# The late stages of a fused attention and gated-MLP training step rebuilt around crossbar loads and tile-wise buffer reuse

## The chip, the cores and the metric

The kernel runs on one core of one Trainium2 chip; the rounds ran on several chips, so ratios are always to the kernel before in the same rounds. The metric is device time in microseconds (us), median of several executions.

## The reference, cut to what matters

Sequence S = 2048, model width D = 576, H = 32 heads of 128, MLP width F = 4608, all bf16. The kernel computes the output of this step and its eight gradients in one launch.

```python
xn  = layernorm(x)
s   = attention(xn @ wq, k_cache, v_cache) @ wo          # O is (S, H*128)
g   = silu((sigmoid(xn @ w_gate) * (xn @ w_up)) @ w_down)
out = x + s * g
# then the vjp of out with grad_out, for x, k_cache, v_cache, wq, wo, w_gate, w_up, w_down
```

## The kernel before: the parts that matter

The program runs in stages, one after another, each with TensorE (PE) as the main engine:

1. gate/up: `xn @ w_gate`, `xn @ w_up`, with `a = sigmoid(g)` and `h = u*a` stored to HBM,
2. down projection,
3. attention forward and backward, head by head,
4. output projection O wo, then `ds`-related elementwise work that makes `doB`, the gradient at the MLP output,
5. MLP gradients, in 18 blocks of 256 columns of F: `dh`, then `du`, `dg`, and the products for dW_down, dW_up, dW_gate,
6. dWo and dWq, in 8 groups of four heads,
7. dx, in 8 blocks of 256 rows, from `du`, `dg` and `dq`.

Gate/up makes `1 - a` by a second sigmoid and stores the product `b = h*(1-a)`, which stage 5 reads back:

```python
nc.scalar.activation(a_row[:, cs], g_ps[:], AF.Sigmoid)
oma = tmpp.tile([P, FCH], bf, name="oma")
nc.scalar.activation(oma[:], g_ps[:], AF.Sigmoid, scale=-1.0)
...                                                      # cut
nc.vector.tensor_tensor(b_row[:, cs], h_row[:, cs], oma[:], op=ALU.mult)
```

The output projection loads `wo` only after attention, turns O on TensorE, and turns the last 64 columns of `B_w_down` on TensorE too (`ldT_tmp`):

```python
nc.sync.dma_start(t_[:], on2_d[st_ * P:(st_ + 1) * P, :])                 # onr
...                                                                      # cut
for j in range(n):
    nc.tensor.transpose(pt[:, j, :], onr[:, (g + j) * P:(g + j + 1) * P], ident[:])
alt.copy(oT[:, g:g + n, :], pt[:, :n, :])
...                                                                      # cut
nc.tensor.matmul(accs[j][:, :nn], lhsT=oT[:, h, :], rhs=wo_sb[:, h, n0:n0 + nn], ...)
```

The MLP gradients form dW_up and dW_gate in the orientation of the output, with 256 moving columns; dWq does the same with 512 columns, per group of four heads:

```python
for i, (d0, kd) in enumerate(dts):                       # five row tiles of D
    for st in range(NT):                                 # 16 tiles of S
        nc.tensor.matmul(acc[:kd, :], lhsT=xn_all[:, st, d0:d0 + kd], rhs=blk_[:, st, :], ...)
...                                                      # cut: stage 6
nc.sync.dma_start(onb[:], on2_d[:, cols]...)             # 2 MB per group, rows of 1 KB
nc.sync.dma_start(dqb[:], dq2_d[:, cols]...)
if hg == min(2, H // HG - 1): load_T_rows(nc, wuT_sb, B_w_up, D)      # crossbar, 5.3 MB
if hg == min(4, H // HG - 1): load_T_rows(nc, wgT_sb, B_w_gate, D)
```

## Time and profile before

The median was 5324.54 us when the prediction was made (3 executions) and 5319.72 us with the profiled one (4 executions, 5310.42 to 5330.38). These are the page's first lines: busy time of TensorE, its share of the span and its instructions.

```profile
span 5319.7 us, 130025 instructions
...
PE 5076.7 (95%) x54342; PEld 3664.5 (69%) x55220; DVE 2681.6 (50%) x6832; ACT 2629.3 (49%) x4678; POOL 920.6 (17%) x1458
```

TensorE is the bound, so a gain must come from fewer or cheaper matmuls or from the 5% in which it waits. The windows view of the kernel before gives the late stages: output projection, MLP gradients, the wait after them, dWo/dWq, dx. Its columns are the stretch, its length, busy time of each engine with instructions in brackets, then the granted TensorE clock, the share of time that the DMA engines were busy, and GB/s.

```profile
core 0: us, PE busy (x) PEld busy (x) DVE busy (x) ACT busy (x) POOL busy (x), PEclk, DMA share, GB/s
3706.00:3951.00 245.00, 185.81 (x1619) 113.47 (x1648) 76.01 (x124) 43.71 (x67) 35.77 (x44) 0.87 0.51 163
3951.00:4600.00 649.00, 637.42 (x5423) 496.10 (x5477) 251.86 (x708) 146.34 (x415) 180.90 (x270) 0.99 0.53 177
4600.00:4617.00 17.00, 0.64 (x3) 0.34 (x4) 0.00 (x0) 0.36 (x1) 0.54 (x1) 0.58 1.14 312
4617.00:4890.00 273.00, 264.10 (x1632) 128.09 (x1662) 28.44 (x52) 24.43 (x52) 39.12 (x72) 0.99 0.58 179
4890.00:5320.00 430.00, 407.04 (x3261) 210.91 (x3326) 45.93 (x128) 13.39 (x64) 8.63 (x16) 0.98 0.71 147
```

The output projection is the weak one: TensorE is busy for 186 of 245 us there. The waits view tells what TensorE waited for (us in total, times, longest), first in gate/up, then from the end of attention on.

```profile
PE g_ps L393 <- ACT oma L399: 21.7, 20, 2.3
```

```profile
PE pt L86 <- DMA ldT_tmp<-in_B_w_down_dram: 23.9, 1, 23.9
PE acc L902 <- DMA onb<-on_d: 16.5, 2, 16.4
PE pt L805 <- ACT oT L40: 15.0, 13, 1.2
...
PE pt L805 <- DVE oT L42: 7.4, 14, 0.6
...
PE accd L860 <- DMA h_blk<-h_d: 5.1, 1, 5.1
```

Four costs stand here that the change means to remove: the second sigmoid (21.7 us), the load of `ldT_tmp` after attention (23.9), the copies of the turned O (15.0 and 7.4), and the wait for `onb` (16.5). Where the last one comes from is seen in the DMA queue of SyncE in the kernel before, around the end of the MLP gradients at 4599.8 us. The columns are the start, how long the entries took in the queue, and what they moved:

```profile
4582.85 0.36 SPq L886 DMA_DIRECT2D ds_all<-ds_d  x1
4583.26 24.68 SPq L92 DMA_TRANSPOSE wuT_sb<-in_B_w_up_dram  x3
4608.25 0.36 SPq L891 DMA_DIRECT2D onb<-on_d  x1
```

The source asks for these weights with the third head group. The scheduler (see below) had put three of the loads ahead of `onb` already here, and one of them waited 13.6 us for the last copy of the stage before. So `onb` was issued 8.5 us after the last matmul of that stage.

### The profile page before, as it was taken

What the parts mean: (1) busy time and instruction counts of PE and PEld (TensorE: products, weight loads), DVE (VectorE), ACT (ScalarE), POOL (GpSimd) and SP (SyncE); (2) the same over time, 40 slices, a digit from 0 to 9 for tenths busy, and PEclk for the clock granted to TensorE, in tenths of its full rate; (3) what the DMA queues carried; (4) which work ended last, traced back from release to release, by engine and by line L of the source; (5) the groups of instructions that cost most, each with busy time, mean ns of one, the idle gap of its engine ahead of it and who ended that gap; (6) DMA issues with size and microseconds to landing.
All of it is one profiled execution on the core that took longest, in us unless ns stands there. A gap on an engine that the chain in (4) does not pass through costs nothing.

```text
span 5319.7 us, 130025 instructions
## 1 busy us (share of the span) xinstructions
PE 5076.7 (95%) x54342; PEld 3664.5 (69%) x55220; DVE 2681.6 (50%) x6832; ACT 2629.3 (49%) x4678; POOL 920.6 (17%) x1458
## 2 busy tenths in 40 slices
PE   8899999999999999999999999998889999899999
PEld 3345777777877877777777777777557777544454
DVE  5744666666665665665665665665334334210011
ACT  7641766766766666666666666665112222100000
POOL 2222111111111111111111111111112232111000
PEclk9999999999999999999999999999899999999999
DMA  7867999999999999999999999999644555765775
GB/s 297 287 208 171 210 203 210 209 210 204 212 213 201 210 207 191 209 211 203 210 200 197 210 213 206 200 201 217 188 153 166 176 185 174 214 197 132 164 149 109
DMA packets 2724762, 1053.95 MB, mean 198 GB/s; under 512 B 2524913, under 2 KB 2645362, under 8 KB 2722114
## 3 DMA queue, kind: packets, MB, share of 16 engines
q1 hardware_dynamic: 2637890, 764.83, 71.9%
q0 software_dynamic: 86272, 280.65, 15.8%
q8 instruction: 433, 7.09, 0.6%
q14 instruction: 167, 1.37, 0.1%
HBM read 213.91 MB, written 201.00 MB: 78 GB/s over the span
## 4 chain that ended last, share of the span: by engine, by line
PE 78%; issue 7%; DMA 4%; SPq 2%; DVE 2%; POOL 1%; ACT 1%; POOLq 0%; DVEq 0%; ACTq 0%
PE acc L637 14%; PE acc L578 14%; PE acc L943 7%; PE sp L531 7%; PE accw L871 6%; PE acc L239 5%; PE dp L601 5%; PE dh L848 3%; PE accd L860 3%; PE acct L176 2%; PE acc L457 2%; PE acc L810 2%; DMA out_dram<-kvo 2%; PE acc L902 2%; PE accq L911 2%
## 5 line engine op out<-in xcount | busy, mean ns | idle before, releaser
L549 ACT ACTIVATE Pq<-sp 128x1024 bf16<-128x1024 f32 x1024 | 1047.1, 1023 | 307.8 <-PE sp L531 194.0
L637 PEld LDWEIGHTS <-Pq 128*128 128x128 bf16 x16384 | 1004.4, 98 | 241.5 <-issue 2.9
L608 ACT ACTIVATE t<-dp,negdelta 128x1024 bf16<-128x1024 f32 x512 | 571.1, 1116 | 222.5 <-PE dp L601 168.9
L604 DVE SCALAR_TENSOR_TENSOR Pq<-dp,negdelta,Pq 128x1024 bf16<-128x1024 f32 x512 | 655.0, 1279 | 42.6 <-PE acc L578 39.6
L578 PEld LDWEIGHTS <-PT 128*128 128x128 bf16 x8192 | 501.9, 98 | 121.6 <-issue 0.3
L601 PE MATMUL dp<-VT,dOT 128*128 128x512 bf16 x1728 | 542.8, 381 | 35.3 <-DVE Pq L604 35.3
L578 PE MATMUL acc<-Kn,dST 128*128 128x128 bf16 x8192 | 552.0, 219 | 7.8 <-DMA dST<-Pq 4.2
L637 PE MATMUL acc<-dOn,Pq 128*128 128x128 bf16 x8192 | 546.1, 219 | 10.1
L578 PE MATMUL acc<-Vn,PT 128*128 128x128 bf16 x8192 | 546.6, 219 | 7.0
L531 PE MATMUL sp<-KT,QT 128*128 128x512 bf16 x1762 | 547.1, 379 | 1.7 <-ACT Pq L549 1.7
L637 PE MATMUL acc<-Qn,Pq 128*128 128x128 bf16 x8192 | 543.3, 220 | 3.4
L578 PEld LDWEIGHTS <-dST 128*128 128x128 bf16 x8192 | 493.0, 98 | 66.4 <-DMA dST<-Pq 5.3
L609 DVE TENSOR_TENSOR Pq<-t,Pq 128x1024 bf16<-128x1024 bf16 x512 | 354.2, 692 | 355.2 <-ACT t L608 348.3
L618 ACT ACTIVATE dq_n<-acc,rsc 128x128 bf16<-128x128 f32 x512 | 188.1, 367 | 336.4 <-PE acc L578 336.4
L651 POOL DMA_DIRECT2D out_dram<-kvo x256 | 140.0, 547 | 1055.8 <-DVE kvo L649 1055.8
L871 PEld LDWEIGHTS <-xn_all 128*128 128x128 bf16 (+1 forms) x2880 | 281.5, 100 | 40.3 <-issue 11.1
L572 POOL DMA_DIRECT2D on_d<-o_n x128 | 97.0, 757 | 737.7 <-DVE junk L590 383.6
L952 ACT ACTIVATE dxn<-acc 128x512 f32<-128x512 f32 (+1 forms) x32 | 12.7, 411 | 413.7 <-PE acc L943 413.7
L649 DVE SCALAR_TENSOR_TENSOR kvo<-acc,part 128x512 bf16<-128x512 f32 x256 | 175.8, 687 | 75.5 <-DMA out_dram<-kvo 42.7
L393 PE MATMUL g_ps<-wg_sb,xnT 128*128 128x512 bf16 x694 | 182.9, 387 | 28.6 <-ACT oma L399 21.7
L957 DVE SCALAR_TENSOR_TENSOR junk<-dxn,xn_all 128x576 f32<-128x576 f32 x16 | 12.1, 753 | 389.4 <-ACT dxn L952 389.4
L601 PEld LDWEIGHTS <-dOT 128*128 128x128 bf16 x2048 | 164.0, 98 | 63.7 <-issue 41.6
(187 smaller groups left out, 7167.8 us busy)
## 6 DMA issues: line engine op xcount, KB each, us to landing
out_dram<-kvo POOLq DMA_DIRECT2D x256, 128.0 KB, 4.1
h_d<-h_row POOLq DMA_DIRECT2D x48, 384.0 KB, 3.5
a_d<-a_row POOLq DMA_DIRECT2D x48, 384.0 KB, 3.7
b_d<-b_row POOLq DMA_DIRECT2D x48, 384.0 KB, 4.1
a_blk<-a_d SPq DMA_DIRECT2D x18, 1024.0 KB, 5.9
b_blk<-b_d SPq DMA_DIRECT2D x18, 1024.0 KB, 18.6
h_blk<-h_d POOLq DMA_DIRECT2D x18, 1024.0 KB, 11.3
du_d<-du_blk POOLq DMA_DIRECT2D x18, 1024.0 KB, 8.9
```

Of the source, the lines that this page charges most:

```text
L239: nc.tensor.matmul(av[:, :CH], lhsT=w[:kk, i, :], rhs=srcT[:kk, i, cs], start=(i == 0), stop=(i == DT - 1))
L531: nc.tensor.matmul(sp[:, c * CH:(c + 1) * CH], lhsT=hs.QT[:, qt * P:(qt + 1) * P], rhs=hs.KT[:, hf * HW_ + c * CH: hf * HW_ + (c + 1) * CH ...
L549: nc.scalar.activation(Pq[:, hsl], sp[:], AF.Exp, scale=SCALE, accum_out=hs.rsp[:, hf:hf + 1])
L578: nc.tensor.matmul(hs.acc[:, 0, :], lhsT=T[:, kt, :], rhs=rhs[:, kt, :], start=(kt == 0), stop=(kt == NT - 1))
L601: nc.tensor.matmul(dp[:, c * CH:(c + 1) * CH], lhsT=hs.dOT[:, qt * P:(qt + 1) * P], rhs=hs.VT[:, hf * HW_ + c * CH: hf * HW_ + (c + 1) * C ...
L604: nc.vector.scalar_tensor_tensor(Pq[:, hsl], dp[:], hs.negdelta[:, qt:qt + 1], Pq[:, hsl], op0=ALU.add, op1=ALU.mult)
L608: nc.scalar.activation(t[:], dp[:], AF.Identity, bias=hs.negdelta[:, qt:qt + 1], scale=1.0)
L609: nc.vector.tensor_tensor(Pq[:, hsl], t[:], Pq[:, hsl], op=ALU.mult)
L618: nc.scalar.activation(hs.dq_n[:, qt % G4, :], hs.acc[:, 0, :], AF.Copy, scale=hs.rsc[:, qt:qt + 1])
L637: nc.tensor.matmul(self.tile[:, j, :], lhsT=self.slabs[qt][:, kt * P:(kt + 1) * P], rhs=self.rhs[:, qt, :], start=(qt == self.lo), stop=(q ...
L871: nc.tensor.matmul(acc[:kd, :], lhsT=xn_all[:, st, d0:d0 + kd], rhs=blk_[:, st, :], start=(st == 0), stop=(st == NT - 1))
L943: nc.tensor.matmul(accs[sl][j][:, :nn], lhsT=ch[:, kk, sl * P:(sl + 1) * P], rhs=wT[:, k0 + kk, n0:n0 + nn], start=(kidx == 0), stop=(kidx ...
```

## The change

Its intent is to take work off TensorE and to load earlier. O^T comes by crossbar loads (DMA that turns a matrix), 1.05 MB for each of 16 tiles. Twenty-six of the 32 row blocks of `wo` are loaded during the last head into four buffers that are dead by then. `B_w_down` is turned wholly by crossbar. The dW and dWq products use pairs of 512 + 64 = 576 moving columns, and the small results are turned back by crossbar. `b` is no longer stored; VectorE makes `nbl = (a-1)*h` in stage 5. The late pools reuse memory tile by tile instead of waiting for a whole stage. Two row blocks of dx run their gate/up passes before `wq` is needed.

```diff
-                oma = tmpp.tile(...); nc.scalar.activation(oma[:], g_ps[:], AF.Sigmoid, scale=-1.0)
-                nc.vector.tensor_tensor(b_row[:, cs], h_row[:, cs], oma[:], op=ALU.mult)
 ...                                                    # cut: last head of attention
+            for view, h0, n, dead in wo_parts:         # dsT, Kn, Vn, dOn are dead here
+                for k in range(0, n, 4):
+                    put(bl + q(at), 0, lambda ...: load_wo_rows(view, h0, k, min(k + 4, n)))
+            put(bl + NT, 0, lambda: load_oT(oT0, 0))   # O^T of tile 0, into the buffer of K and Q
 ...                                                    # cut: output projection
-                    nc.tensor.transpose(pt[:, j, :], onr[...], ident[:])   # 512 in all, and copies
+                if st + 1 < NT:
+                    load_oT(oTs[(st + 1) % 2], st + 1)         # crossbar, two buffers
+                for _ in range(NWD if st else 0):              # one piece per tile from tile 1 on
+                    nc.sync.dma_start_transpose(wdT_sb[:, i, r0:r0 + WH], B_w_down[...])
+                if st == min(2, NT - 1):
+                    nc.gpsimd.dma_start(xn_all[:], xn_d[...])  # 2.3 MB, plain
 ...                                                    # cut: MLP gradients
-                    for i, (d0, kd) in enumerate(dts):         # 80 matmuls of 256 columns
-                        nc.tensor.matmul(acc[:kd, :], lhsT=xn_all[:, st, d0:d0+kd], rhs=blk_[:, st, :])
+                    for fl in range(FB // P):                  # 2 x 16 pairs of 512 + 64 columns
+                        accumulate(psa, blk_, xn_all, lcols, dwT, "acc")
+                        nc.sync.dma_start_transpose(stg_[:, :, lcols], dwT[:])
+                    store_T(out_, fcols, stg_)                 # plain stores, POOL queue
 ...                                                    # cut: dWo/dWq
+            dqTs = padded(wp, 2, "dqT")
+                    accumulate(ps, dqb, xn_all, lcols, dqTs[h % 2], "acc")
+                    nc.sync.dma_start_transpose(dwq[:, :, lcols], dqTs[h % 2][:])
+                    if hg >= min(1, H // HG - 1):
+                        wT_piece()                             # one of 10 crossbar loads of wuT, wgT
```

The program is put in order by a scheduler: an instruction may be issued earlier on its queue than the source has it, as soon as its buffers allow.

## The prediction

> **What bounds the kernel now.** TensorE: the page gives PE 95% of a 5319.7 us span, clock 0.985. Stages (start times in the source-line view): gate/up 0–379 us, down projection –534, attention –3706, output projection (O wo) –3951, MLP gradients –4602, dWo/dWq –4885, dx –5320. The change leaves attention (3172 us, PE 98% busy in the windows view) alone except for prefetches in its last head; about 2150 us can change.
>
> **Where that part loses PE time.**
> - After attention PE idles 24 us (3706–3730, "ldT_tmp<-in_B_w_down_dram" 23.9). The 512 onr transposes cost 46 us busy plus waits for the oT copies (22 us). The stage takes 245 us, while 512 pairs (512+64 columns) at 0.246 us (60 matmuls took 7.4 us in the timeline) need 126.
> - MLP gradients: 80 dW matmuls of 256 columns took 8.95 us; 32 pairs instead need 7.9. 36 such products: −39 us. Start wait for h_blk and slow first block: about −9.
> - dWq: a 4-head group took 33.2 us; 64 of its pairs need 15.7, so the 80 matmuls of 512 take 17.5. With 64 pairs: −1.8 us × 8 = −14. The 16.5 us wait for onb at this stage's start goes with tile-wise reuse.
> - Start of dx: PE busy 55 of 75 us (4885–4960) while weights and chunks load. Two row blocks now run their gate/up passes before wq is needed: about −10, tail about −2, and the 5 us gap before it goes.
> - Gate/up: PE busy 333.6 of 379; 21.7 us wait for oma (ACT), which disappears with b_row and the b_d stores: −15 to −20.
>
> **What it adds.** VectorE: nbl, 288 × about 0.33 us (estimate from 1.21 us for the 1024-column form of this operation). The built order puts most of them in the dW phase, where VectorE idles. Not critical. Crossbar turns of dW: 72 × 0.16 MB, small.
>
> The output projection becomes transpose-bound at first: 15 oT loads of 1.05 MB and ten pieces of B_w_down of 0.59 MB. In the trace transposes with DMA share above 1 ran at about 206–295 GB/s in all (4885–4920). The Trainium skill, "DMA: Bandwidth & Descriptors", Latency and other measured facts, states 261 GB/s effective for DMA transposes; the trace agrees roughly. In the built order two pieces precede the second oT and five the fourth, beside about 7 MB of plain loads. I estimate 20–30 us of PE waits among tiles 1–5. Stage: 131 + 25 + 3 = 159 us (−86).
>
> **Sum (us):** gate/up −17, output projection −86, MLP gradients −48, dWo/dWq −33, dx −10: −194. Predicted 5131 us, range 5085–5190 (80%). Chances: faster by over 2% 0.93, within 2% 0.06, slower 0.01.
>
> **What would show it.** PE idle after attention falls from 24 us to under 5; the stage's PE waits name DMA oT/KQ<-on_d, only in early tiles; no pt<-onr transposes; MLP gradient block period falls from 35.4 to about 33.3 us, its stage to about 600; a dWo/dWq group from 33.2 to 31.4 us; gate/up ends near 362 us; attention lasts 3172 ± 10.
>
> **What would make it wrong.** oT transposes slower than estimated beside plain loads (every tile waits: +40 us); nbl pushing VectorE past PE in the dh phase (up to +4 us × 18); a pair with changing weights slower than 0.246 us; the granted clock falling as PE idles less; attention disturbed by the wo prefetches.

## The result, and the profile after

The changed kernel gives correct results and takes 5240.31 us (median of 4, 5231.27 to 5251.32), against 5319.72 us. The ratio is 0.9851, with a 95% interval of 0.9823 to 0.9879. Such a ratio is the mean time of one kernel's fast runs over that of the other's of the same rounds, so it is not quite the ratio of the medians. The gain is 1.5%; 3.6% was predicted, and the time lies outside the range.

The profiled execution was the slowest of the four (5251.32 us), so its stages add up to a little more than the median. The page of the changed kernel:

```profile
span 5249.3 us, 127878 instructions
...
PE 4959.8 (94%) x53585; PEld 3490.0 (66%) x54480; DVE 2580.0 (49%) x6718; ACT 2600.7 (50%) x4663; POOL 901.3 (17%) x1373
```

TensorE lost 117 us of busy time (5076.7 to 4959.8), but the span only 70: its idle time grew from 243 to 289 us. The same five stretches of the windows view as above, for the changed kernel:

```profile
3717.00:3916.00 199.00, 137.99 (x1086) 71.94 (x1106) 43.06 (x61) 18.95 (x44) 36.80 (x46) 0.87 0.92 196
3916.00:4501.70 585.70, 580.45 (x4836) 359.68 (x4908) 265.96 (x868) 185.64 (x506) 147.52 (x179) 1.00 0.62 177
4501.70:4535.40 33.70, 0.34 (x4) 0.03 (x1) 0.00 (x0) 0.70 (x2) 7.45 (x10) 0.53 1.13 291
4535.40:4811.60 276.20, 251.66 (x2007) 130.08 (x2048) 0.00 (x0) 44.37 (x128) 41.96 (x59) 0.96 0.75 182
4811.60:5249.00 437.40, 408.65 (x3261) 210.80 (x3328) 50.34 (x128) 14.29 (x64) 18.52 (x34) 0.98 0.73 147
```

In the output projection TensorE idles as long as before (61 us against 59), while the DMA share rose from 0.51 to 0.92. The wait before dWo/dWq doubled, and inside that stage TensorE idles 24.5 us where it idled 9.

The lengths below are read from the first and last starts of each stage's matmuls in the trace. The output projection includes the gap after attention, and dWo/dWq includes the wait ahead of it.

| stage | before, us | after, us | measured change | predicted change |
|---|---|---|---|---|
| gate/up | 379.7 | 379.4 | -0.3 | -17 |
| down projection | 155.2 | 153.0 | -2.2 | 0 |
| attention | 3171.1 | 3185.2 | +14.1 | 0 |
| output projection | 245.0 | 198.9 | -46.1 | -86 |
| MLP gradients | 648.8 | 585.3 | -63.5 | -48 |
| dWo/dWq | 16.6 + 273.3 | 33.7 + 276.2 | +20.0 | -33 |
| dx | 430.0 | 437.6 | +7.6 | -10 |
| sum | 5319.7 | 5249.3 | -70.4 | -194 |

The waits of TensorE in the changed kernel, in gate/up and then from the end of attention on:

```profile
PE g_ps L363 <- DMA wg_sb<-in_B_w_gate_dram: 15.0, 3, 12.2
PE g_ps L363 <- ACT a_row L366: 12.3, 9, 2.6
PE u_ps L365 <- DVE h_row L369: 9.6, 10, 4.3
```

```profile
PE acc L842 <- DMA onb<-on_d: 33.5, 1, 33.5
PE acc L813 <- DMA oTb<-on_d: 25.3, 5, 19.6
PE acc L842 <- ACT dqT L40: 20.9, 1, 20.9
PE acc L813 <- DMA wo_x<-in_A_wo_dram: 19.4, 1, 19.4
PE acc L964 <- DMA cg<-dg_d: 9.3, 3, 7.0
PE pt L58 <- DVE doB L820: 7.4, 2, 6.8
```

Three of the four old waits are gone. The fourth, for `onb`, has doubled (16.5 to 33.5 us), and three new single stalls of 19 to 21 us have come. Each can be followed in the DMA queues. First SyncE's in the output projection of the changed kernel:

```profile
3717.90 6.56 SPq L786 DMA_TRANSPOSE wdT_sb<-in_B_w_down_dram  x2
3724.81 5.05 SPq L470 DMA_TRANSPOSE oTb<-on_d  x1
3749.85 6.70 SPq L470 DMA_TRANSPOSE KQ<-on_d  x1
3756.60 25.64 SPq L786 DMA_TRANSPOSE wdT_sb<-in_B_w_down_dram  x5
3782.35 4.90 SPq L470 DMA_TRANSPOSE oTb<-on_d  x1
```

Five pieces of `B_w_down` stand ahead of the O^T of tile 3 and take 25.6 us; TensorE waits 19.6 us for it. The stall for `wo_x`, the six row blocks of `wo` that found no dead buffer, comes in tile 0: in the trace their load is issued at 3726.26 us on POOL's queue, right behind the 2.3 MB of `xn_all` (3725.10) and ahead of the two first blocks of stage 5, 1 MB each.

Then the start of dWo/dWq, in SyncE's queue and in POOL's (in brackets, how long POOL idled before, and for what):

```profile
4520.58 69.30 SPq L63 DMA_TRANSPOSE wgT_sb<-in_B_w_gate_dram  x5
4590.14 10.76 SPq L926 DMA_TRANSPOSE dwq<-dqT  x5
```

```profile
4507.17 0.76 POOL L850 DMA_DIRECT2D out_dram<-dwu  x1 [19.27 <-DMA dwu<-dwT]
...
4521.27 0.77 POOL L850 DMA_DIRECT2D out_dram<-dwg  x1 [11.45 <-DMA dwg<-dwT]
...
4522.74 1.19 POOL L916 DMA_DIRECT2D onb<-on_d  x1
```

The source asks for the weight loads one by one, from the second head group on. The scheduler put all ten ahead, amid and behind the last turns of the MLP gradients, and so ahead of the first turn of dWq. So POOL's stores of dW_up and dW_gate wait for turns that stand behind weights (19.27 and 11.45 us), and the loads of `ds_all` and `onb`, which stand behind those stores, are issued late. Then five weight loads take 69.3 us. The first turns of dWq stand behind them, and with two `dqT` buffers TensorE stops for 20.9 us.

### The profile page after: what moved, and what is told of

It is laid out like the page before. It is cut to its first block, busy times and chain, and to the rows that moved or that the text cites. A ratio compares the mean times of both kernels' runs of the same rounds, so it can differ in the third digit from the quotient of the medians.

```text
span 5249.3 us, 127878 instructions
## 1 busy us (share of the span) xinstructions
PE 4959.8 (94%) x53585; PEld 3490.0 (66%) x54480; DVE 2580.0 (49%) x6718; ACT 2600.7 (50%) x4663; POOL 901.3 (17%) x1373
## 4 chain that ended last, share of the span: by engine, by line
PE 79%; issue 7%; DMA 6%; SPq 3%; DVE 2%; POOL 1%; ACT 1%; POOLq 0%; DVEq 0%; ACTq 0%
PE acc L622 15%; PE acc L563 14%; PE acc L842 12%; PE acc L964 7%; PE sp L516 7%; PE dp L586 5%; PE acc L212 5%; PE dh L872 3%; PE acct L145 2%; PE u_ps L365 2%; PE g_ps L363 2%; PE acc L425 2%; SPq L63 2%; DMA out_dram<-kvo 2%; PE acc L813 1%
## 5 line engine op out<-in xcount | busy, mean ns | idle before, releaser
L622 PE MATMUL acc<-dOn,Pq 128*128 128x128 bf16 x8192 | 546.9, 219 | 10.1
L516 PE MATMUL sp<-KQ 128*128 128x512 bf16 x1762 | 548.4, 380 | 2.8 <-ACT Pq L534 2.7
L50 DVE TENSOR_SCALAR o_n<-acc,rinv_all 128x128 bf16<-128x128 f32 x352 | 123.4, 351 | 168.2 <-PE acc L563 168.2
```

The source lines that it names most:

```text
L516: nc.tensor.matmul(sp[:, c * CH:(c + 1) * CH], lhsT=hs.QT[:, qt * P:(qt + 1) * P], rhs=hs.KT[:, hf * HW_ + c * CH: hf * HW_ + (c + 1) * CH ...
L622: nc.tensor.matmul(self.tile[:, j, :], lhsT=self.slabs[qt][:, kt * P:(kt + 1) * P], rhs=self.rhs[:, qt, :], start=(qt == self.lo), stop=(q ...
```

## The experiments

Sixteen runs were made, and all gave correct results. Each is the changed kernel with the edit shown, unless said otherwise. "Anchor" below means that one column of a load's destination is first written from a late result, so that the scheduler cannot issue the load before that result is there. The values are overwritten by the load, so the results stay right. Times are medians, and ratios are to the kernel before in the same rounds; the changed kernel's own ratio is 0.9851 in its rounds. Only the ratios of e4, e7, e10, e11 and e13 differ from it clear of noise.

Stage lengths and waits are read from one profiled execution of each run. How far they scatter is seen in the runs that leave a stage alone. The output projection took 189.8 to 206.8 us in eight of them, dWo/dWq with its wait 294.0 to 309.9 in nine, gate/up 377.8 to 382.4, dx 437.3 to 440.8, and the MLP gradients 585.3 almost always. In the nine profiles of dWo/dWq the first wait for `onb` was 32.4 to 33.5 us, but the wait for `dqT` 4.2 to 20.9. The changed kernel's own profile, with 309.9 and 20.9, is the longest of them.

### e1: the weight loads of dWo/dWq behind a result of their own head

```diff
-                        wT_piece()
+                        wT_piece(dwo[:, 0:1])   # anchor
```

> The ten crossbar loads of the gate and up weights each wait for a dWo tile of their own head (from the second head group on), the bytes are the same. Theory (order): in the changed kernel these loads stand in the in-order SP queue ahead of the turns of the last dW products and of the first dWq products; the dW stores and the onb load behind them in the in-order POOL queue wait for those turns (PE wait 33.5 us), and the two dqT buffers wait for turns behind five loads (20.9 us). Then the first wait falls to 8-15 us (ds_all and onb must still land), the second to under 2, the stage from the last dW to the first dx matmul goes from 310 to 268-275 us, and the whole from 5240 to about 5200. Rival (bandwidth): the DMA engines are full there whatever the order; the waits only move, the stage stays above 300 us.

Measured: 5235.53 us, ratio 0.9839 (0.9823 to 0.9856). The wait at the start fell from 33.7 to 20.0 us, not to the 8 to 15 that were expected; the rest of the stage stayed (276.9). TensorE still waited 19.8 us for `onb` and 19.0 us for `dqT`. So the place of the weights is part of the first wait, but not the whole of it. The sum of 296.9 us lies within the scatter.

### e2: the stores of dW_up and dW_gate on SyncE's queue

```diff
-            nc.gpsimd.dma_start(out_[...], stg_...)
+            nc.sync.dma_start(out_[...], stg_...)     # these two stores only
```

> Only the stores of the turned dW go to the SP queue instead of the POOL queue, so that no store waiting for a turn stands ahead of the onb and ds_all loads. Theory (order, POOL part): onb is issued right after the last dW matmuls, about 15 us earlier, and the PE wait at the start of dWo/dWq falls from 33.5 to 15-22 us; the 20.9 us wait for dqT stays; total about -12 to -18 us. If the POOL queue is not what holds onb (rival: DMA bandwidth, or memory not yet free), the wait stays above 28 us.

Measured: 5235.45 us, ratio 0.9841 (0.9825 to 0.9858). The first wait fell to 6.3 us, as POOL no longer waits for turns before it issues `ds_all` and `onb`. But the `dqT` wait grew from 20.9 to 32.6 us. The stage with its wait came to 294.7 us, which is within the scatter, so no gain of the whole stage is shown. The saved time was handed to the next entry of the same queue: the five loads of `wgT` still stood ahead of the first dWq turns.

### e3: six dqT buffers instead of two

```diff
-            dqTs = padded(wp, 2, "dqT")
+            dqTs = padded(wp, 6, "dqT")
```

> Six instead of two buffers for the untransposed dWq products, nothing else. Theory (order): the 20.9 us PE wait in dWo/dWq is for a buffer whose turn is queued behind the gate-weight loads; with six buffers it goes to 0-3 us and the 33.5 us wait stays; total about -18 us. Rival (bandwidth): the next head group's loads are late too and the wait reappears under their name; total within 5 us of the changed kernel.

Measured: 5241.86 us, ratio 0.9852 (0.9836 to 0.9869). The `dqT` wait is gone, the first wait is not (32.4 us), and a wait that the changed kernel had only as 6.4 us in four parts stands at the start of dx:

```profile
PE acc L964 <- DMA cu<-du_d: 19.4, 1, 19.4
```

In SyncE's queue two chunks of `dq` and the last turn now stand ahead of this chunk, which starts at 4783.97 us, 8.5 us after the last matmul of the stage. The author's reading is that the larger pool moved the memory layout, so that the first chunk of dx came to lie over the `dqT` buffers. The gain in this stage was lost at the next. The later runs give `dqT` a pool of its own, and there this wait does not come (e10: 6.5 us in five parts).

### e4: the pieces of B_w_down one per tile

```diff
+                        nc.vector.tensor_copy(wdT_sb[:, i, r0:r0 + 1], s_prev[:, 0:1])   # anchor: tile before
                         nc.sync.dma_start_transpose(wdT_sb[:, i, r0:r0 + WH], ...)
 ...                                                    # cut: the O^T load of tile 2 is anchored on tile 0
```

> In the output projection each of the ten B_w_down pieces waits for the tile before, as the source has it written (one a tile), and the load of tile 2 waits for tile 0, so the SP queue alternates oT and piece; bytes are the same. Theory (order): the 19.6 us wait of tile 3 (five pieces ahead of its oT) goes, oT waits in this stage fall from 25 to under 10 us in all, the 19.4 us wait for wo_x stays or shrinks a little; stage 196 to about 175-180 us, total -15 to -20. Rival (bandwidth): the transposes of this stage (about 22 MB) cannot keep up with PE, the waits spread over tiles 1 to 11, stage within 8 us of 196.

Measured: 5214.88 us, ratio 0.9795 (0.9774 to 0.9816). The output projection fell from 198.9 to 172.2 us; the stall of 19.6 us is gone:

```profile
PE acc L816 <- DMA oTb<-on_d: 13.9, 6, 6.5
PE acc L816 <- DMA wo_x<-in_A_wo_dram: 7.6, 1, 7.6
```

In the changed kernel the scheduler had bunched the pieces, so their place was the larger part of the loss. But of the gain of 26.7 us only 11.4 is wait for `oTb` (25.3 to 13.9). The waits for `wo_x` and `doB` fell by 11.8 and 6.8 us too, though their loads are in POOL's queue; that the pieces no longer take DMA time from them is likely but not shown alone (`wo_x` was 10.1 to 22.8 us in the runs that leave this stage alone).

### e5: the plain loads later, the pieces as they were

```diff
+                    nc.vector.tensor_copy(xn_all[:, 0, 0:1], s_prev[:, 0:1])             # anchor
                     nc.gpsimd.dma_start(xn_all[:], xn_d[...])
+                    # the same anchor for a_first and h_first
```

> In the output projection the plain loads of xn_all (2.3 MB) and of the first activation blocks (2 x 1 MB) wait for a tile's result as the source places them, so the wo rows of the last six heads (wo_x, 0.9 MB) are first in the POOL queue after attention. Theory (order): the 19.4 us PE wait for wo_x in tile 0 was time behind these 4.4 MB and falls to under 8 us; the 19.6 us wait of tile 3 behind five pieces stays or shrinks a little; stage 199 to about 180-187 us, total -12 to -18. Rival: wo_x is late because it is loaded only after attention at all, whatever follows it; then the wait stays above 14 us.

Measured: 5238.88 us, ratio 0.9851 (0.9816 to 0.9886). The `wo_x` wait fell from 19.4 to 8.2 us (10.1 to 22.8 in the runs that leave this stage alone), so the big plain loads issued around it made most of it. The stage took 195.1 us, which is within the scatter, because tile 3 then waited 21.0 us behind the bunched pieces. A stall that is taken away ahead of another hands its time on.

### e12: e4 and e5 together

Both edits as shown, nothing else.

> Both edits of the output projection: wo_x first in its queue, and one B_w_down piece a tile behind the oT load. With wo_x alone first, its wait had fallen from 19.4 to 8.2 us but tile 3 then waited 21 us behind the five pieces, so the stage kept its length (195 against 199). Theory (order): both waits go together, stage 199 to 160-168 us, total -31 to -39 against the changed kernel. Rival (bandwidth): the stage stays at the 172 us that the pieces alone gave.

Measured: 5221.25 us, ratio 0.9817 (0.9795 to 0.9839). The stage took 180.2 us, more than with e4 alone. The expectation from order alone fell. `wo_x` cost only 1.8 us, but one wait of 19.9 us for `oTb` was back, now in a queue with the right order. This is SyncE's queue of that run; `xn_all` was issued beside these two entries:

```profile
3737.01 14.52 SPq L470 DMA_TRANSPOSE oTb<-on_d  x1
3751.58 13.66 SPq L789 DMA_TRANSPOSE wdT_sb<-in_B_w_down_dram  x1
```

Other entries of the same two kinds took 4.7 to 5.2 and 2.3 to 5.9 us in this part of the trace. That suggested contention with the plain load; e13 tests it.

### e7: the old 256-column form of dW in the changed kernel

```diff
-                        accumulate(psa, blk_, xn_all, lcols, dwT, "acc")     # and its crossbar turn
+                        nc.tensor.matmul(acc[:kd, :FB], lhsT=xn_all[:, st, d0:d0 + kd], rhs=blk_[:, st, :], ...)
```

> In the MLP gradients the up and gate products are computed in the form of before (80 matmuls of 256 columns, no turn), everything else of the change stays. If the gain of this stage came from moving 576 columns (theory), the stage goes from 585 to 585 + 36 x (8.95 - 7.85) = about 625 us, and the rest of its gain over the 650 of before (about 24 us) is the prefetched blocks, the deeper buffers and the missing b_blk load. If the gain came from those alone (rival), the stage stays below 600. The turns also vanish, so if turns behind weight loads hold the stores of the last dW (order theory), the 33 us wait at the start of dWo/dWq falls below 20 us.

Measured: 5269.42 us, ratio 0.9902 (0.9877 to 0.9927). The stage took 625.3 us. So the 576-column pairs are worth 40.0 us (625.3 - 585.3), near the 39 of the prediction. The other 23.5 us of the gain (648.8 - 625.3) come from the rest of the change in this stage. TensorE idles 1.3 us in e7's stage against 11.6 before, which accounts for 10.3 of them; the remaining 13.2 us are less busy time, part of it a granted clock of 1.00 against 0.99. The first wait of dWo/dWq fell to 16.8 us without the turns, close to the 16.6 before: the turns standing among weight loads made the other half of it. The `dqT` wait grew to 29.8 us in exchange.

### e8: the row blocks of dx in another order

```diff
-                            if wq_pieces and self.k:           # wq among the first chunks
+                            if wq_pieces and self.sbi == 1:    # wq only from the second row block, anchored
 ...                                                    # cut: the first cq chunk is anchored behind the cg chunks
```

> At the start of dx the wq pieces come only with the second row block's chunks and the first cq chunk after its gate chunks; bytes are the same. Theory (order): the 20 us that PE loses between 4811 and 4900 (waits for cu and cg behind a cq chunk and five wq pieces) fall to under 10, the dx stage from 438 to about 427 us, total -8 to -12. Rival (bandwidth): about 16 MB of transposes in 73 us is more than the crossbar gives; the wait moves to the chunks of the second row block or to wq, stage within 4 us of 438.

Measured: 5234.87 us, ratio 0.9823 (0.9797 to 0.9849). dx took 435.1 us against 437.6, and its waits for chunks fell from 16.7 to 9.7 us. The runs with the older order took 437.3 to 440.8 us and the three with this one 433.9 to 435.1, so the order is worth 2 to 7 us; it explains part of the missing gain in dx at most.

### e6: the load of w_down where the source has it

```diff
+                            nc.vector.tensor_copy(wd_sb[:, 0, 0:1], xn_st[:, NT - 1, 0:1])   # anchor
                             nc.gpsimd.dma_start(wd_sb[:], B_w_down...)
```

> The 5.2 MB load of the down weights, issued 9 us after the start in the changed kernel (11 us in the one before) in the middle of the first gate and up weights, waits for the last normalized tile as the source has it. Theory: the gate/up stage lost its expected gain (379.4 against 379.7 us) because the weights of its first products land later, PE idle 24.5 us in its first 40 us against 16.3 before; with the load moved the idle falls to 12-16 us and the stage to 367-372 us, total -8 to -12. Rival: the later part, where PE waits behind sums of squares that wait for the key cache, takes it back; stage stays above 376.

Measured: 5232.76 us, ratio 0.9840 (0.9821 to 0.9859). The scheduler had issued this load of 5.3 MB at 9 us. With it later, TensorE's idle time in the first 40 us fell from 24.5 to 11.9 us, but in the stretch from 80 to 120 us it rose from 3.1 to 14.0, where the load now runs (DMA share 0.93). Gate/up took 375.2 us: nearer to the rival (above 376) than to the theory (367 to 372). The load cost at its new place most of what it had cost at the old one. Whether it would be free between 40 and 80 us, where the DMA share is now 0.42, was not tested.

### e9: O^T of tile 0 loaded later in the last head

```diff
+                    nc.vector.tensor_copy(oT0[:, 0, 0:1], heads[H - 1].negdelta[:, NT - 1:NT])   # anchor
                     load_oT(oT0, 0)
```

> The crossbar load of the first O^T tile (1 MB) goes behind the last probability transposes of the last head instead of ahead of the last two. Theory: the 7.1 us PE wait for PT in the last head goes, attention 3185 to about 3174-3178 us, and the first tile of the output projection still does not wait for it; total -5 to -8. Rival: attention is longer for another reason (clock), the change stays within 3 us.

Measured: 5247.23 us, ratio 0.9862 (0.9840 to 0.9883). In the trace the load moved from 3659.7 to 3680.8 us, yet attention took 3187.6 us. The theory that this load lengthens attention fell.

### e10: e1 and e2, the dWq stores on SyncE too, and six dqT buffers in a pool of their own

```diff
+                        wT_piece(dwo[:, 0:1])                              # as in e1
+        with ... late("c2d") as dqp, ...:                                  # a pool for dqT alone
-            dqTs = padded(wp, 2, "dqT")
+            dqTs = padded(dqp, 6, "dqT")
+                store_T(out_4, cols, dwq, eng=nc.sync)                     # and dwu, dwg as in e2
```

> The three edits for dWo/dWq together: weight transposes one a head from the second head group on, stores of turned products in the SP queue, six dqT buffers (in a pool of their own, so that the first dx chunks do not lie over them; in the run with six buffers a 19.4 us wait for the first dx chunk had appeared in place of the removed one). Theory (order): both waits go, first wait 6-10 us, no dqT wait, the time from the last dW to the first dx matmul falls from 310 to 258-265 us, total -45 to -52 against the changed kernel, which also says that single edits gained only 15 each because each left the other wait longer. Rival (contention): transposes beside the 2 MB loads of 1 KB rows are so slow (14 to 32 us each seen) that new waits for onb, dqb or chunks appear; more than 275 us.

Measured: 5201.70 us, ratio 0.9769 (0.9735 to 0.9803). The wait fell to 2.7 us and the stage to 252.9: 255.6 us against 309.9 after and 289.9 before. The `dqT` wait does not occur, and the remaining wait for `onb` is 2.5 us. That is 34.3 us below the kernel before; the prediction had -33. Busy time in the stage fell from 264.4 to 250.6 us, 13.8 where the prediction had 14 for the columns, and the first wait by 13.9 where it had 16.5; the rest is idle time inside the stage. So the arithmetic of this term was right, and queue order and buffer count had taken it. What each of the edits gives alone in this company was not tested.

### e11: all of e1, e2, e4, e5, e6, e8, e9, e10

No edit is new here; the `dqT` buffers have their own pool as in e10.

> All edits together (both of the output projection, the three of dWo/dWq, the order at the start of dx, the late down-weight load, the late first O^T tile). Theory: the gains add up, since each names a wait of another place: output projection -33, dWo/dWq -54, gate/up -8, attention -6, dx -3 = -104 us, 5240 to 5136 us (5120 to 5155), faster than both kernels by over 2% against before (ratio 0.962 to 0.970). Rival: stages hand waits to each other or the clock falls as PE idles less; 5165 us or more.

Measured: 5176.59 us (5171.99 to 5208.99, 6 executions), ratio 0.9744 (0.9720 to 0.9768), faster than both kernels. But the gains did not add up: 5136 us was expected, and the rival (5165 or more) held. The output projection took 179.5 us with the same 19.7 us wait for `oTb` as in e12, and the MLP gradients 591.3 us.

### e13: e11 with xn_all at tile 11 and the first blocks at tile 13

```diff
-                if st == min(2, NT - 1):           # xn_all
+                if st == min(11, NT - 1):
-                if st == NT // 2:                  # a_first, h_first
+                if st == min(13, NT - 1):
```

> All earlier edits together, with xn_all (2.3 MB) loaded at tile 11 and the first blocks of the gradient stage at tile 13, after the last piece of B_w_down has been turned, instead of tile 2 and tile 8. Contention theory (the load of xn_all slows the crossbar load of O^T for tile 3): the wait for oTb in tile 3, 19.9 us in the version with all edits, falls below 8 us, the stage from the end of attention to the first dW group falls from 179.5 to 160 to 168 us, and the time to about 5162 us. Rival (the crossbar loads of O^T and of B_w_down are too slow by themselves beside the small g2b, dsb, xb and gob loads): the stage stays above 175 us and the oTb waits move to other tiles. A third possibility is that the late loads are themselves waited for at the start of the gradient stage: then the wait for a_first or xn_all is over 5 us there.

Measured: 5163.29 us (5158.99 to 5180.39, 5 executions), ratio 0.9723 (0.9704 to 0.9742). SyncE's order is that of e11, entry by entry. The entries that took 14.5 and 13.7 us in e12 read:

```profile
3737.44 4.98 SPq L471 DMA_TRANSPOSE oTb<-on_d  x1
3742.47 8.56 SPq L793 DMA_TRANSPOSE wdT_sb<-in_B_w_down_dram  x1
```

The O^T load falls to 5 us as soon as the plain load is elsewhere, and no `oTb` wait is over 4.9 us. The contention theory holds for that stall. The DMA packets in the traces, counted by queue, show how: in e12 SyncE's queue moved 185 GB/s from 3731 to 3740 us, while POOL's moved nothing, and 18 GB/s from 3743 to 3752, while POOL's moved 256. In that second stretch the two queues moved about as many packets (646 and 539), but a crossbar packet had 256 bytes and a plain one 4275 on average. The counts fit two queues that take turns packet by packet when both have work, so that the crossbar gets little.

But the stage fell to 172.3 us only, not to 160 to 168, and e4 alone, with `xn_all` at its old place, had reached 172.2: waits of 17.2 us for `oTb` and 8.4 us for `KQ` remain in eleven small parts. An O^T load and a piece together take 7 to 14 us in this queue in the first tiles, and the 64 matmuls of a tile about 7.9 us (32 pairs at 0.245), so in most of the tiles with pieces the crossbar, not TensorE, sets the pace. The late loads were not waited for, and the MLP gradients took 585.3 us again.

### e14 and e16: the loads of wo out of the last head

Every profile of a changed kernel up to here shows TensorE waiting 4.1 to 7.5 us for turned blocks (`PT`) in the last head; the kernel before does not. e14 asked for the `wo` loads after the last step instead of during it:

```diff
-                    put(bl + q(at), 0, lambda ...: load_wo_rows(...))
+                    put(bl + NT, 0, lambda ...: load_wo_rows(...))
```

> The changed kernel with one edit: the 26 wo row loads into dead buffers are issued after the last main step of the last head instead of during it. If they are what delays the PT turns (7.1 us of PE wait in the profile of after) and so lengthens attention, the PT wait in the last head goes to under 1.5 us and attention lasts 3173 to 3178 us instead of 3185; c1 then waits for wo and starts later, so the total gets longer by 5 to 15 us. Rival (the longer attention is scatter of the granted clock from run to run): the PT wait goes but attention stays anywhere in 3170 to 3188 us.

Measured: 5232.95 us (2 executions), ratio 0.9843 (0.9823 to 0.9862), attention 3190.2 us, a `PT` wait of 5.3 us. In its trace the loads into `dsT` start at 3620.9 us, amid the last head as before. The scheduler had put them back. e16 gives each of them an anchor on dQ of query tile 8:

```diff
+                if hs.h == H - 1 and qt == NT // 2:
+                    for view, h0, a, b in late_wo:
+                        nc.vector.tensor_copy(view[:, a, 0:1], hs.dq_n[:, 0, 0:1])
+                        load_wo_rows(view, h0, a, b)
```

> The run with the wo loads moved in program order did not test what it meant to: its trace shows that the scheduler put them back, all but one small one, where they were (3621 us, amid the last head). Here each of these loads first needs one column written from a late result of the last head (dQ of query tile 8), so they stand near its end. If the wo loads delay the PT turns of the last head and the stall lets the clock down, the PT wait (7.1 us in the profile of after, 5.3 in the earlier try) goes to under 2 us, the window of 98 us from 3038 us after the start of attention shows PE busy 94 to 96 us at clock 0.99 or more (before: 95.4 and 95.9; after: 89.8), and attention gets about 5 us shorter than the 3183 us mean of the changed kernels. Rival (another cause, such as the shared tile of K and Q or the clock itself): the window stays at 89 to 92 us of PE busy. In both, the output projection starts later or waits for wo and the total does not get shorter by more than 5 us.

Measured: 5235.78 us (2 executions), ratio 0.9841 (0.9812 to 0.9869). Now the loads start at 3687.3 us and the `PT` wait is gone altogether. These are ten microseconds of the windows view at the place of the stall, in the changed kernel and then in e16:

```profile
3630.00:3640.00 10.00, 2.88 (x28) 2.32 (x28) 1.02 (x6) 2.23 (x6) 0.76 (x1) 0.68 1.19 182
3640.00:3650.00 10.00, 9.90 (x112) 7.95 (x112) 6.22 (x30) 5.58 (x11) 0.00 (x0) 0.81 1.26 241
```

```profile
3628.00:3638.00 10.00, 10.00 (x140) 8.24 (x138) 7.20 (x36) 7.79 (x16) 0.76 (x1) 1.00 1.05 217
3638.00:3648.00 10.00, 10.00 (x143) 8.35 (x141) 6.39 (x29) 8.05 (x15) 0.76 (x1) 1.00 1.04 209
```

In the window of 98 us from 3038 us after the start of attention, TensorE is busy 96.8 us at clock 1.00 in e16, 89.8 us at 0.95 in the changed kernel, and 95.4 us at 1.00 before. So the `wo` loads make this stall, and the clock falls with it. Attention still took 3182.8 us, because the loads then ran beside the last turns of dS and TensorE waited 9.8 us there. Wherever they stand in the last head, these loads delay a crossbar turn that TensorE needs soon.

### e15: the kernel before once more

No edit.

> The kernel before, unchanged, for a second profile of its attention stage. If the 14 us by which attention is longer in the profile of after is scatter of runs, this profile shows attention at 3175 us or more (the first showed 3171); if the change lengthens attention it is within 3168 to 3173 us again.

Measured: 5328.25 us, one execution of unknown state. Attention took 3171.5 us, as in the first profile (3171.1). Its window in the last head showed 95.9 us busy. Fifteen profiles of changed kernels before e16 show 88.6 to 92.0 us there. Attention of the changed kernels ranges from 3170.1 to 3190.2 us, so a single profile of it tells little, but the loss in the last head is no scatter.

## Why the prediction was wrong, point by point

The direction was right and the size was not: 194 us predicted, 70.4 in the profiles. The 124 us between are these terms, each from one profile of either kernel; the scatter given above is to be kept in mind.

**dWo/dWq, 53 us (predicted -33, measured +20).** The step that failed was "The 16.5 us wait for onb at this stage's start goes with tile-wise reuse." It took the wait for one of memory alone. The kernel before shows a matter of queue order: `onb` stood behind three weight loads, and the change left weights ahead of it by another way. Ten weight loads now stood among and ahead of the turns, and the wait for `onb` became 33.5 us by way of POOL's stores (e2: 6.3 once those stores leave POOL). The two `dqT` buffers stalled TensorE for 20.9 us behind the weights (4.2 to 20.2 in the other profiles of this stage; e3 and e10: none). By the nine profiles the term is +4 to +20. With both mended it is -34.3 us (e10). The columns themselves did what was costed.

**Output projection, 40 us (predicted -86, measured -46).** The built order was read rightly (five pieces ahead of the fourth O^T), and "I estimate 20–30 us of PE waits among tiles 1–5" nearly held for the waits that it meant: 25.3 us for `oTb` and 4.8 for `KQ`. The step that failed was "the stage's PE waits name DMA oT/KQ<-on_d, only in early tiles": plain loads were waited for too. TensorE waited 19.4 us for `wo_x` in tile 0 and 7.4 for `doB`, which the sum had at nothing. Busy time was 138 us instead of 131, at a granted clock of 0.87. e4 shows that the bunched pieces were worth most of it (199 to 172 us), e5 and e12 (8.2 and 1.8 us) that the plain loads made most of the `wo_x` stall, and e13 that an O^T load takes 5 us instead of about 15 once the load of `xn_all` is moved away from it. The prediction's 159 us was not reached by any version; the best is 172.

For the speed of these loads the prediction leaned on the Trainium skill, "DMA: Bandwidth & Descriptors", section "Latency and other measured facts", which gives 261 GB/s for transposing DMAs with a non-contiguous middle dimension and about 350 to 400 for contiguous ones; the prediction left that condition out. The traces show less. By the packets of the changed kernel, SyncE's queue moved 223 GB/s from 4490 to 4510 us, while POOL's moved 7. Beside plain loads it was far less: 22 GB/s from 4530 to 4545 us, while POOL's queue moved 380. So the five loads of `wgT` (5.3 MB) took 69.3 us, 77 GB/s (46.0 to 69.3 us in the nine profiles), and the O^T load of e12 72 GB/s. The same skill, "Trainium Kernel Development and Optimization", section "Key Constraints", says that DMAs issued from the three queues run on the same 16 engines and interleave. The traces agree, but the shares are far from even (22 against 380 GB/s). With a DMA share of 0.92 in this stage, the plain loads should have been counted against the crossbar loads.

**Gate/up, 17 us (predicted -17, measured -0.3).** "21.7 us wait for oma (ACT), which disappears" was right: it is gone. What failed is "−15 to −20", the step from a wait to the stage. TensorE now waits 15.0 us for `wg_sb` and 21.9 us for `a_row` and `h_row`, in a stage whose DMA share is 0.96 in its first 40 us. e6 moved one load and gained 4.2 us. e6 supports that DMA sets the pace in the stretch where that load runs, not that it bounds the whole stage (share 0.39 after 240 us); where the remaining `a_row` waits come from in detail was read, not tested.

**dx, 18 us (predicted -10, measured +7.6).** "Two row blocks now run their gate/up passes before wq is needed: about −10" failed. It rests on "PE busy 55 of 75 us (4885–4960)"; the trace of the kernel before has 60.6, so 14.4 us were to be had, not 20. And TensorE's waits for chunks of `du`, `dg` and `dq` in dx grew from 8.8 to 16.7 us. e8's other order gained 2.5 us only. All loads through the crossbar at that point (the last dWq turns, `wq`, the chunks) go through one queue, and e11 and e13 brought 434 us. The two profiles of before gave 430.0 and 431.8, those of changed kernels 433.9 to 440.8, and e3's 427.4, ahead of which the 19.4 us wait stands. The cause is not settled.

**Attention, 14 us (predicted 3172 ± 10, measured 3185).** The prediction named "attention disturbed by the wo prefetches" as a risk and gave it nothing in the sum. e16 shows that these loads cost 5 to 8 us at their place, and move the cost when moved. From 686 to 882 us after the start of attention the profiled execution has a second dip: TensorE is busy 186.4 us there against 192.9 and 192.0 before. Other changed kernels show 184.6 to 192.3, so part of it is scatter; no run explains it.

**MLP gradients, 15 us the other way (predicted -48, measured -63.5).** The step "80 dW matmuls of 256 columns took 8.95 us; 32 pairs instead need 7.9" held: 40.0 us in e7 against 39. The mis-sized term was "Start wait for h_blk and slow first block: about −9": it measured 23.5, of which 10.3 is idle time. The risk named for `nbl` did not come: it took 0.42 us each instead of 0.33, and TensorE's waits for `dh` are under 1 us in all.

The sizes add up to 53 + 40 + 17 + 18 + 14 - 15 = 127 us, and the down projection gave back 2.2; that the sum is 124 and not 125 is rounding. The clock was named as a risk too: it was 0.981 after and 0.985 before in the mean. The Trainium skill, "TensorE: Matmul & The Clock Gate", section "What's actually happening", says that the clock follows how busy TensorE has been lately. The traces agree: the stretch with the `PT` stall shows 0.68, the next ten microseconds 0.81, then 1.00; the wait of 33.7 us before dWo/dWq shows 0.53. A stall therefore costs a little more than its length: the product after the 20.9 us stall took 5.39 us, the others 4.08.

## What to carry to other kernels

When work moves from TensorE to crossbar loads, draw up each queue in its built order before counting a gain. Ask of every load what stands ahead of it, what plain loads run beside it, and which buffer frees it: ten weight loads ahead of small turns, with two buffers, turned a gain of about 33 us into a loss of 4 to 20. Give each load that is needed later a true dependence, because source order alone does not hold it back, and check in the trace that an experiment moved what it meant to move. Before a wait is put down to memory, look in the queue for what stood ahead of the load. Freeing memory sooner is no gain by itself: in these runs the transfers that then started first were not those that were needed first.

The version that follows from the runs is e13: 5163.29 us, ratio 0.9723 to the kernel before. Against the changed kernel's 0.9851 that is about 1.3% (0.9723 / 0.9851 = 0.987); the two ratios are of different rounds. e11's 0.9744 is not clear of e13's.

## What the Trainium skill lacked or had wrong

- "DMA: Bandwidth & Descriptors", "Latency and other measured facts", gives 261 GB/s for transposing DMAs with a non-contiguous middle dimension, and 350 to 400 for contiguous ones. Here the queue of crossbar loads moved 223 GB/s with almost nothing beside it. The row gives no figure for plain loads beside them: 22 GB/s against 380 for 15 us, 77 GB/s for 5.3 MB of weights, and 14.5 us instead of 5.0 for an O^T load beside the 2.3 MB of `xn_all`. The trace's packets (250 bytes against 4004 on average in those 15 us, 1295 and 1424 of them) fit two queues that take turns packet by packet.
- "Trainium Kernel Development and Optimization", "Key Constraints", says that the queues share the DMA engines, and the runs agree. The line does not add that a queue also holds back whatever stands behind a waiting entry (that engine queues are first in, first out is said elsewhere in the skill): POOL's loads stood behind stores that waited 19.27 and 11.45 us for crossbar turns, and moving those stores alone took the first wait of the next stage from 33.7 to 6.3 us.
- No page has a warning that a scheduler may issue a load earlier than the source has it, and so undo an experiment: loads that were asked for after the last step started at 3620.9 us, amid the head, and only a written column moved them (to 3687.3).
